# Attention and token mixture on one core: every mixture product and attention score as one float32 matmul, without the split into halves

## The chip, the core and the metric

The kernel runs on one core of a Trainium2 chip. The metric is the device time of the whole program in microseconds (us). Five engines matter: TensorE (PE in the profile; PEld is its loading of the stationary operand), VectorE (DVE), ScalarE (ACT), GpSimd (POOL) and SyncE (SP, which here only issues transfers).

## The reference

Eight batches, eight heads each, 576 tokens, head size 64. Attention keeps only the scores within `tau` of the row's maximum; its output `x` (576 x 512 per batch) goes through a mixture that turns each channel by an angle, mixes tokens, and adds a clipped channel product.

```python
scores = scale * np.matmul(q, k.transpose(0, 1, 3, 2))
thresh = np.max(scores, axis=-1, keepdims=True) - tau
scores = np.where(scores >= thresh, scores, -1000000000.0)
attn = np.exp(scores - max); attn = attn / (sum(attn) + 1e-09)
x = attn @ v                          # heads side by side: (8, 576, 512)
theta = x @ w_theta
y = w_tok_r @ (x * cos(theta)) + w_tok_i @ (x * sin(theta))
u = x + y
out = u + np.maximum(u @ w_ch, 0.0)
```

All inputs are float32 or float64 and the results float32; the mixture's weights and scores have to be held to nearly float32 accuracy.

## The kernel before

**Attention.** Two heads make a pair; there are 32 pairs, four to a batch. A pair is cut into nine *halves*: for query blocks i = 0 to 3 of 128 rows one half for each of the two heads, and one half for the 64 last rows of both heads together (i = 4). `score` computes one half: 128 queries against 576 keys, in two pieces of 288 columns (`h`), into one PSUM tile `s_ps` of which there is a single buffer. VectorE then negates it into SBUF and takes the row minimum (`sc`, L282), ScalarE takes the exponential (L299), and VectorE masks it and sums the rows (L300). `flip` and `flip_last` turn the result with TensorE transposes (`t_ps`), ScalarE copies it out (`a`), and `values` multiplies it with `v` into `o_ps`, with the two heads in the two halves of the output partitions (64 columns of the array each). `invert` and `normalize` bring 1/sum to the layout of `xT` by five transposes (`rb_ps`, `rl_ps`) and VectorE multiplies.

**Operands in two parts.** TensorE's operands for scores, products and token sums are of type fp32r, and each float32 operand is split into a high part (a cast) and a low part (the rest). A key gives `k1`, `k2`; a query has its high part in partitions 0 to 63 and its low part in 64 to 127 of one tile, so that two matmuls give all four products of parts. Every product of the mixture is three matmuls: high x high, low x high, high x low.

```python
def split(eng_hi, eng_lo, hi, lo, src):
    copy(eng_hi, hi, src)
    eng_lo.tensor_tensor(out=lo, in0=src, in1=hi.bitcast(F32), op=ALU.subtract)
...
terms = ((0, 0), (1, 0), (0, 1))                      # product: 12 matmuls for each h
...
work = [(zz[c][0], w[:, c, hs]) for c in range(NK) for w in (wt_h, wt_l)]
work += [(zz[c][1], wt_h[:, c, hs]) for c in range(NK)]   # token: 27 matmuls for each h
```

**Mixture.** `moe(b)` works on blocks m = 0 to 3 of 128 channels: `angle` (a product with `w_theta`, then VectorE reduces the angle: `km`, L453), `sines` (ScalarE sine and cosine for two m at once, between two table loads, and GpSimd multiplies them with `x`, L483), `flip` (nine transposes for each m), `token` (`y_ps`), and four products with `w_ch`. The string `ORDER` sets their sequence. `split_x` and `split_u` split `x` and `u`; the split weights of the products lie in DRAM and are fetched again by a GpSimd DMA for each m.

**Order of the work.** TensorE runs in the order in which the code is written. `score` is called three halves ahead. After each score and after each flip, `fill()` puts in pieces of the mixture of the batch before, as many as a cost budget allows (`share` per call, less the number that each piece yields). So there are nine stretches: the attention of batch 0 alone, with the conversion of the weights (`load_weight`: float64 to float32 on ACT, DVE and PE); then seven rounds of one batch's attention with the mixture of the batch before; and the last mixture alone. The other engines' order is set by a list scheduler, by priorities and its own estimate of the times.

Of the kernel before, what the change touches and what calls it, by code (L numbers as in the profile page):

```python
# [10 lines left out]
F32 = mybir.dt.float32  # L11
F32R = mybir.dt.float32r
# [4 lines left out]
DRAM = bass.MemoryType.DRAM  # L17
# [16 lines left out]
LAG = 3  # L34
# [5 lines left out]
def tile_attn_moe(  # L40
# [12 lines left out]
    B, NP, D, _, S = qT.shape  # L53
# [4 lines left out]
    SP = S + 64  # L58
    NK = 9
# [3 lines left out]
    dram = ctx.enter_context(tc.tile_pool(name="dram", bufs=1, space=DRAM))  # L63
# [27 lines left out]
    wt_h = const.tile([P, NK, S], F32R, name="wt_h")  # L91
    wt_l = const.tile([P, NK, S], F32R, name="wt_l")
    wm_dram = dram.tile([2, NM, P, 2, NM, P], F32, name="wm_dram")

    def pool_copy(out, in_):
        nc.gpsimd.tensor_scalar(out=out, in0=in_, scalar1=1.0, scalar2=0.0, op0=ALU.mult, op1=ALU.add)

    def copy(eng, out, in_):
        if eng is nc.scalar:
            nc.scalar.copy(out=out, in_=in_)  # L100
        elif eng is nc.gpsimd:
            pool_copy(out, in_)
        else:
            eng.tensor_copy(out=out, in_=in_)  # L104

    def split(eng_hi, eng_lo, hi, lo, src):

        copy(eng_hi, hi, src)
        eng_lo.tensor_tensor(out=lo, in0=src, in1=hi.bitcast(F32), op=ALU.subtract)  # L109
# [10 lines left out]
    turn = [0]  # L120

    def load_weight(src, n, on_pe=True):

        w = pool.tile([P, S], F32, tag="xh", name="w", bufs=4)[:, :n]
        if src.dtype == F32:
            nc.sync.dma_start(w, src)
            yield
            return [(slice(0, n), w)]
        turn[0] += 1
        tag, bufs = ("wm", 3) if turn[0] % 2 else ("z", 3)  # L130
        raw = pool.tile([P, S, 2], U32, tag=tag, name="wraw", bufs=bufs)[:, :n]
        nc.sync.dma_start(raw, src.bitcast(U32).rearrange("p (n t) -> p n t", t=2))
        low, high = raw[:, :, 0], raw[:, :, 1]
        bits = pool.tile([P, S], U32, tag="xh", name="bits", bufs=4)[:, :n]
        mag = pool.tile([P, S], U32, tag="xl", name="mag", bufs=4)[:, :n]
# [11 lines left out]
        nc.vector.tensor_scalar(out=mag, in0=bits, scalar1=0xFF800000, scalar2=None, op0=ALU.bitwise_and)  # L147
        nc.vector.scalar_tensor_tensor(out=w, in0=low, scalar=2.0**-52, in1=magf, op0=ALU.mult, op1=ALU.mult)
        if not on_pe:
            nc.vector.tensor_tensor(out=w, in0=w, in1=bitsf, op=ALU.add)  # L150
            yield
            return [(slice(0, n), w)]
# [3 lines left out]
        got = []  # L156
        for c in range(0, n, n2):
# [3 lines left out]
            got.append((slice(c, c + n2), ps))  # L161
        return got

    def load_wtok(c):
        got = yield from load_weight(w_tok[c * P : (c + 1) * P, :], S)
        for r, w in got:
            split(nc.scalar, nc.vector, wt_h[:, c, r], wt_l[:, c, r], w)

    def load_wm(which, src, c):
        got = yield from load_weight(src[c * P : (c + 1) * P, :], DM, which == 0)  # L170
        hi, lo = (pool.tile([P, DM], F32R, tag="zh4" if x == "whi" else "zl4", name=x, bufs=4) for x in ("whi", "wlo"))
        for r, w in got:
            split(nc.scalar, nc.vector, hi[:, r], lo[:, r], w)
        for i, t in enumerate((hi, lo)):
            nc.sync.dma_start(
                wm_dram[which, :, :, i, c, :].rearrange("m p e -> p m e"),
                t.bitcast(F32).rearrange("p (m e) -> p m e", e=P),
            )
# [11 lines left out]
    def get_wm(which, m):  # L190
# [19 lines left out]
    def load_raw(n, src, name, j):  # L210
        raw = temp(name)
        for r in (slice(0, 64), slice(64, P)):
            nc.sync.dma_start(raw[r], src[n // NP, n % NP, :, j])
# [486 lines left out]
```

## Time and profile before

| | |
|---|---|
| median of 3 runs | 1151.37 us (1150.37 to 1155.16) |
| span of the profiled execution | 1147.4 us |
| around the span (median less span) | 4.0 us |
| TensorE busy | 1043.9 us, 91% |
| VectorE busy | 869.0 us, 76% |
| ScalarE busy | 750.0 us, 65% |
| GpSimd busy | 375.1 us, 33% |
| mean granted TensorE clock | 0.981 |
| mean DMA rate | 92 GB/s |

No own time of the profiled execution is given beside its span; it is taken as the span and the 4.0 us that the median lies above it.

How to read it: matmuls are pipelined, and a matmul's shown duration (around 0.3 us) contains its passage through the array; what one costs TensorE is the distance to the next start. In the chain of waits, pieces of consecutive matmuls follow each other without overlap, so that a piece's time over its count is that distance. The list of groups by line shows a matmul once for each instruction that TensorE executed; a matmul on float32 operands is two instructions there, one on fp32r is one.

### The profile page before, as it was taken

The numbers are of one execution on the slowest core, as the hardware profiler recorded it, in microseconds if no ns is written. First come the engines' busy times: TensorE is split into PE (matmuls) and PEld (weight loads), VectorE is DVE, ScalarE is ACT, GpSimd is POOL, SyncE is SP. The second block draws the span as 40 slices with busy tenths as digits, with TensorE's granted clock in tenths as the row PEclk, the third lists the DMA queues.
The fourth block names the chain that finished last, engine by engine and source line by source line (L and its number), as shares of the span: only waits on it lengthen the run. The fifth ranks groups of instructions, "written<-read, shape, count | busy, mean of one in ns | idle before, by whom it ended". The sixth has DMA issues, their size and how long they took to land.

```text
span 1147.4 us, 21175 instructions
## 1 busy us (share of the span) xinstructions
PE 1043.9 (91%) x7736; PEld 921.5 (80%) x7736; DVE 869.0 (76%) x2139; ACT 750.0 (65%) x1394; POOL 375.1 (33%) x303
## 2 busy tenths in 40 slices
PE   4888888799899998999979998999989999799998
PEld 3566687688779987898869987799878998689898
DVE  7998777987877677876787768776788678787362
ACT  6766869666676566964677666865678656774350
POOL 2203325233342243521443234422435314430210
PEclk9999999999999998999999999999999999999999
DMA  7722223255231052213432142311522133310421
GB/s 252 213 81 84 64 71 97 88 138 148 76 100 53 28 178 74 79 47 103 116 100 63 32 146 76 102 53 34 173 87 72 43 113 104 97 32 1 120 71 60
DMA packets 55176, 105.26 MB, mean 92 GB/s; under 512 B 11936, under 2 KB 20128, under 8 KB 55072
## 3 DMA queue, kind: packets, MB, share of 16 engines
q1 hardware_dynamic: 45856, 70.35, 20.9%
q0 software_dynamic: 9216, 33.56, 10.2%
q8 instruction: 61, 1.00, 0.4%
q14 instruction: 43, 0.35, 0.1%
HBM read 90.24 MB, written 13.63 MB: 91 GB/s over the span
## 4 chain that ended last, share of the span: by engine, by line
PE 64%; DVE 15%; ACT 13%; issue 4%; DMA 2%; POOL 1%; SPq 0%; ACTq 0%; POOLq 0%; DVEq 0%
PE y_ps L512 15%; PE m_ps L405 13%; PE o_ps L361 13%; PE s_ps L278 11%; PE t_ps L326 7%; DVE sc L282 3%; DVE s_sb L300 3%; DVE km L453 3%; ACT s_sb L299 3%; DMA qraw<-in_qT_dram 2%; ACT a L331 2%; PE rb_ps L377 1%; PE z_ps L495 1%; ACT z L471 1%; ACT z L472 1%
## 5 line engine op out<-in xcount | busy, mean ns | idle before, releaser
L300 DVE SCALAR_TENSOR_TENSOR s_sb<-sc,nm,s_sb 128x576 f32<-128x576 f32 x288 | 276.1, 960 | 69.4 <-ACT s_sb L299 65.5
L299 ACT ACTIVATE s_sb<-sc,nm 128x576 f32<-128x576 f32 x288 | 224.1, 778 | 110.8 <-DVE sc L282 109.9
L278 PE MATMUL s_ps<-k,qq 128*128 128x288 f32 (+1 forms) x1344 | 240.2, 307 | 53.8 <-DVE sc L282 39.8
L282 DVE TENSOR_SCALAR_CACHE_REDUCE sc<-s_ps 128x576 f32<-128x576 f32 x288 | 216.7, 753 | 67.2 <-PE s_ps L278 64.3
L278 PEld LDWEIGHTS s_ps<-k,qq 128*128 128x128 f32 x1344 | 193.8, 192 | 81.4 <-DVE sc L282 46.6
L361 PE MATMUL o_ps<-a,v 128*64 128x320 f32 (+1 forms) x1280 | 180.2, 430 | 31.2 <-DVE nm L295 27.7
L331 ACT COPY a<-t_ps 128x512 f32<-128x512 f32 x256 | 148.2, 579 | 58.2 <-PE t_ps L326 56.9
L326 PE MATMUL t_ps<-ident,s_sb 128*128 128x128 f32 x1152 | 175.4, 275 | 1.7 <-DVE zl L498 1.7
L361 PEld LDWEIGHTS o_ps<-a,v 128*64 128x64 f32 x1280 | 92.5, 143 | 97.8 <-ACT s_sb L299 30.4
L512 PE MATMUL y_ps<-wt_h,zh 128*128 128x288 f32 x576 | 165.2, 305 | 6.3 <-DVE zl L498 4.8
L512 PE MATMUL y_ps<-wt_l,zh 128*128 128x288 f32 x576 | 163.0, 301 | 0.0
L109 POOL TENSOR_TENSOR k<-kraw,k 128x576 fp32r<-128x576 f32 x62 | 90.8, 1465 | 202.4 <-ACT k L100 201.0
L228 POOL TENSOR_TENSOR qq<-qraw,qq 64x576 fp32r<-64x576 f32 x62 | 95.1, 1534 | 159.9 <-ACT qq L226 130.4
L326 PEld LDWEIGHTS t_ps<-ident,s_sb 128*128 128x128 f32 x1152 | 142.4, 142 | 3.8 <-DVE zl L498 1.9
L512 PEld LDWEIGHTS y_ps<-wt_h,zh 128*128 128x128 f32 x576 | 108.6, 188 | 8.1 <-DVE zl L498 6.2
L512 PEld LDWEIGHTS y_ps<-wt_l,zh 128*128 128x128 f32 x576 | 108.6, 189 | 0.0
L512 PE MATMUL y_ps<-wt_h,zl 128*128 128x288 f32 x576 | 103.6, 306 | 0.0
L192 POOL DMA_DIRECT2D wm<-wm_dram x64 | 36.4, 570 | 171.0 <-PE m_ps L405 142.6
L405 PE MATMUL m_ps<-xh,wm 128*128 128x288 f32 x512 | 91.5, 305 | 0.3 <-ACT xh L100 0.3
L483 POOL TENSOR_TENSOR z<-z,xT 128x576 f32<-128x576 f32 x56 | 80.0, 1457 | 31.5 <-ACT z L471 31.4
L109 POOL TENSOR_TENSOR ul<-xT,uh 128x576 fp32r<-128x576 f32 x24 | 34.7, 1448 | 169.8 <-DVE uh L104 169.8
L405 PE MATMUL m_ps<-uh,wm 128*128 128x288 f32 x512 | 84.0, 299 | 0.0
(85 smaller groups left out, 1641.9 us busy)
## 6 DMA issues: line engine op xcount, KB each, us to landing
wm<-wm_dram POOLq DMA_DIRECT2D x64, 512.0 KB, 4.0
qraw<-in_qT_dram SPq DMA_DIRECT2D x128, 144.0 KB, 2.9
kraw<-in_kT_dram SPq DMA_DIRECT2D x128, 144.0 KB, 2.9
out_dram<-xT SPq DMA_DIRECT2D x32, 288.0 KB, 2.2
v<-in_vp_dram SPq DMA_DIRECT2D x32, 256.0 KB, 2.7
wraw<-in_w_tok_dram SPq DMA_DIRECT2D x9, 576.0 KB, 5.0
wraw<-in_w_theta_dram SPq DMA_DIRECT2D x4, 512.0 KB, 4.4
wm_dram<-whi SPq DMA_DIRECT2D x8, 256.0 KB, 2.3
```

The lines of the kernel that those rows point to most:

```text
L109: eng_lo.tensor_tensor(out=lo, in0=src, in1=hi.bitcast(F32), op=ALU.subtract)
L228: eng.tensor_tensor(out=qq[64:128], in0=raw[64:128], in1=qq[64:128].bitcast(F32), op=ALU.subtract)
L278: nc.tensor.matmul(ps[:, h, d0:d1], st, kk, start=(x == 0), stop=(x == len(todo) - 1))
L282: nc.vector.tensor_scalar(out=sc.rearrange("p (a b) -> p a b", a=2), in0=ps[:, :, :HS], scalar1=-1.0, scalar2=None, op0=ALU.mult, op1=ALU.min,
L299: nc.scalar.activation(out=e, in_=u.ps[j], func=AF.Exp, bias=nm[:, j : j + 1], scale=-1.0)
L300: nc.vector.scalar_tensor_tensor(out=e, in0=u.ps[j], scalar=nm[:, 2 + j : 3 + j], in1=e, op0=ALU.is_le, op1=ALU.mult, accum_out=u.pr.rows[ ...
L326: nc.tensor.transpose(out=tp[:, c * P : (c + 1) * P], in_=u.sf[:, k0 + c * P : k0 + (c + 1) * P], identity=ident)
L331: nc.scalar.copy(out=t.a[:, :, j, q0 : q0 + P], in_=tp.rearrange("p (c q) -> p c q", c=4))
L361: nc.tensor.matmul(o[64 * j : 64 * j + 64, :w], st, mv, start=(c == 0), stop=(c == 4))
L405: nc.tensor.matmul(tiles[h][:, :HS], wm[:, a, c, :], parts[c][bb][:, hs], start=(count[h] == 0), stop=(count[h] == 11))
L483: lo_eng.tensor_tensor(out=zi, in0=zi, in1=x, op=ALU.mult)
L512: nc.tensor.matmul(ps[:, :HS], z, w, start=(n == 0), stop=(n == len(work) - 1))
```

## The change

- `score`: the two heads' keys lie stacked in the 128 partitions of one float32 tile `k` (the second head's turned by 64 columns, as before), and a query tile holds one head's queries in its 64 partitions and zeros in the other 64. One float32 matmul per `h` replaces two fp32r matmuls. For i = 4, whose query columns hold both heads, a second key tile `k4` with both heads' keys unturned is loaded.
- `prepare_q`, `prepare_k`: transfers go straight into these tiles; of the splits only the scaling of the queries by `gate` stays, on ScalarE (one instruction for both heads).
- `product`, `token`: one float32 matmul for each block instead of three fp32r ones: 4 instead of 12, and 9 instead of 27. `split`, `split_x`, `split_u`, the low parts `zl`, the weights' trip through DRAM and `get_wm` go; the weights `wt`, `wm` stay in SBUF in float32.
- `normalize`: the copy `rb` on ScalarE goes; ten float32 matmuls of 64 columns spread 1/sum instead of five transposes of 128 columns, and one VectorE multiply instead of two closes the last columns.
- The costs that `fill` counts: 242 for each float32 matmul in place of 131 for each fp32r one; `share` follows.

```diff
 def load_weight(src, out, on_pe=True):
...
             nc.tensor.matmul(ps, ident, bitsf[:, c : c + n2], start=True, stop=False)
             nc.tensor.matmul(ps, ident, w[:, c : c + n2], start=False, stop=True)
-            got.append((slice(c, c + n2), ps))
+            nc.scalar.copy(out=out[:, c : c + n2], in_=ps)
 def load_wtok(c):
-        for r, w in got:
-            split(nc.scalar, nc.vector, wt_h[:, c, r], wt_l[:, c, r], w)
+        yield from load_weight(w_tok[c * P : (c + 1) * P, :], wt[:, c])
...
+    def prepare_q(n):
+        pr = pairs[n] = SimpleNamespace(n=n, b=n // NP, p=n % NP, a={})
+        pr.qf = qq_t[n % 2]
+        for j in range(2):
+            r = slice(64 * j, 64 * j + 64)
+            mine = pr.qf[r, S * j : S * j + S]
+            nc.sync.dma_start(mine, qT[pr.b, pr.p, j])
...
+            nc.scalar.activation(out=pr.qf, in_=pr.qf, func=AF.Copy, scale=gate)
+    def prepare_k(n):
+        pr.k = pool.tile([P, S], F32, tag="k", name=f"k{n}", bufs=3)
+        nc.sync.dma_start(pr.k, kT[pr.b, pr.p, 0:2].rearrange("j d s -> (j d) s"))
+        pr.k4 = pool.tile([P, S], F32, tag="k4", name=f"k4{n}", bufs=2)
+        for j in range(2):
+            nc.sync.dma_start(pr.k4[64 * j : 64 * j + 64], kT[pr.b, pr.p, 2 * j])
...
 def score(u, j):
-            parts = [(pr.qf[:, c : c + P], j, kk, 0) for kk in pr.keys[j]]
...
-                nc.tensor.matmul(ps[:, h, d0:d1], st, kk, start=(x == 0), stop=(x == len(todo) - 1))
+        c = 512 if u.i == 4 else u.i * P + SP * j
+        k = pr.k4 if u.i == 4 else pr.k
         for h in range(2):
+            nc.tensor.matmul(ps[:, h, :HS], pr.qf[:, c : c + P], k[:, h * HS : (h + 1) * HS], start=True, stop=True)
...
 def normalize(pr):
-        for i in range(4):
-            nc.tensor.transpose(out=tp[:, i * P : (i + 1) * P], in_=pr.rb[:, i * P : (i + 1) * P], identity=ident)
+        for i in range(5):
+            for j in range(2):
+                r = slice(64 * j, 64 * j + 64)
+                if i < 4:
+                    out, col, eye = tp[r, i * P : (i + 1) * P], 2 * i + j, ident
+                else:
+                    out, col, eye = tl[r, :64], 8, ident[:, r]
+                nc.tensor.matmul(out, pr.rows[:, col : col + 1].broadcast_to([P, 64]), eye, start=True, stop=True)
...
 def product(w, m, xs, todo, together):
-            runs = [[(h, *t, c) for t in terms for c in range(NM)] for h in range(2)]
+            runs = [[(h, c) for c in range(NM)] for h in range(2)]
...
-                    yield 131 * (len(run) if len(run) < 12 else 4)
+                if n == len(run) - 1 or n % 2 == 1:
+                    yield 242 * (n % 2 + 1)
...
 def flip(m):
-                nc.scalar.copy(out=zh, in_=tv)
-                nc.vector.tensor_tensor(out=zl, in0=tv, in1=zh.bitcast(F32), op=ALU.subtract)
+                nc.scalar.copy(out=zt[:, c0 : c0 + nb], in_=tp[:, : nb * P].rearrange("p (c q) -> p c q", q=P))
 def token(m):
-                for n, (z, w) in enumerate(work):
-                    nc.tensor.matmul(ps[:, :HS], z, w, start=(n == 0), stop=(n == len(work) - 1))
-                    if n % 3 == 2:
-                        yield 393
+                for c in range(NK):
+                    nc.tensor.matmul(ps[:, :HS], zt[:, c], wt[:, c, hs], start=(c == 0), stop=(c == NK - 1))
+                    if c % 2 == 1 or c == NK - 1:
+                        yield 242 * (1 + c % 2)
...
-    share = (16 * 3 * 524 + 4 * 990 + 72 * 393) / (per - 1) / 2
+    share = (64 * 242 + 4 * 990 + 72 * 242) / (per - 1) / 2
```

How the order moves, at two places on which the prediction rests.

TensorE, in a round, while one block's `token` runs between the scores and flips of the attention. Before, a score is four rows and the token sum alternates between the weights' two parts; the step shown ends at the next score:

```order
L278 MATMUL s_ps<-k_15_0_5752,qq_85 128x288
L278 MATMUL s_ps<-k_15_0_5753,qq_85 128x288
L278 MATMUL s_ps<-k_15_0_5752,qq_85 128x288
L278 MATMUL s_ps<-k_15_0_5753,qq_85 128x288
L512 MATMUL y_ps<-wt_h,zh 128x288
L512 MATMUL y_ps<-wt_l,zh 128x288
L512 MATMUL y_ps<-wt_h,zh 128x288
L512 MATMUL y_ps<-wt_l,zh 128x288
L512 MATMUL y_ps<-wt_h,zh 128x288
L512 MATMUL y_ps<-wt_l,zh 128x288
L512 MATMUL y_ps<-wt_h,zh 128x288
L512 MATMUL y_ps<-wt_l,zh 128x288
```

The same engine in the same kind of place after the change:

```order
L221 MATMUL s_ps<-k_3920,qq_81 128x288 x2
L430 MATMUL y_ps<-wt,zt 128x288 x3
L269 MATMUL t_ps<-ident,s_sb 128x128 x4
L284 MATMUL t_ps<-ident,s_sb 128x128
L430 MATMUL y_ps<-wt,zt 128x288 x2
L221 MATMUL s_ps<-k_3920,qq_81 128x288 x2
```

The sequence of scores, mixture pieces and flips is the same; a score is two written matmuls, and four or five token matmuls stand in a step where there were about fifteen. Over the whole program the matmuls of 288 columns go from 1216 (and 64 pairs of 224 and 64 columns), 1536 and 1728 for scores, products and token sums to 576, 512 and 576.

VectorE, in the attention of batch 0 after the weights are done (pair 3; `sc` is a score leaving PSUM, `s_sb` the masked exponential, `nm` a small instruction on the row minimum). Before, the score of the next half stands ahead of the mask of this one:

```order
L282 TENSOR_SCALAR sc,nm<-s_ps 128x576
L300 SCALAR_TENSOR_TENSOR s_sb,rows_1095<-sc,nm,s_sb 128x576
L295 TENSOR_SCALAR nm<-nm,small 128x1
L282 TENSOR_SCALAR sc,nm<-s_ps 128x576
L300 SCALAR_TENSOR_TENSOR s_sb,rows_1095<-sc,nm,s_sb 128x576
L295 TENSOR_SCALAR nm<-nm,small 128x1
L282 TENSOR_SCALAR sc,nm<-s_ps 128x576
L300 SCALAR_TENSOR_TENSOR s_sb,rows_1095<-sc,nm,s_sb 128x576
```

The same engine and place after the change:

```order
L225 TENSOR_SCALAR sc,nm<-s_ps 128x576
L238 TENSOR_SCALAR nm<-nm,small 128x1
L243 SCALAR_TENSOR_TENSOR s_sb,rows_632<-sc,nm,s_sb 128x576
L225 TENSOR_SCALAR sc,nm<-s_ps 128x576
L238 TENSOR_SCALAR nm<-nm,small 128x1
L243 SCALAR_TENSOR_TENSOR s_sb,rows_632<-sc,nm,s_sb 128x576
L225 TENSOR_SCALAR sc,nm<-s_ps 128x576
L238 TENSOR_SCALAR nm<-nm,small 128x1
```

After the change, each half's three instructions follow each other, so that VectorE stands in its queue before the mask until ScalarE has this half's exponential. The same pattern holds in most of the rounds.

More of the change, by code (lines that the diff above doesn't have):

```diff
@@ L52, in tile_attn_moe @@
     nc = tc.nc
-    B, NP, D, _, S = qT.shape
+    B, NP, _, D, S = qT.shape
     P = 128
@@ L58, in tile_attn_moe @@
     SP = S + 64
+    assert D == 64 and S == 576
     NK = 9
@@ L89, in tile_attn_moe @@
     nc.vector.memset(half_pi, 0.5 * math.pi)
[L91 to L109, printed above, removed]
+    wt = const.tile([P, NK, S], F32, name="wt")
+    wm = [const.tile([P, NM, DM], F32, name=f"wm{i}") for i in range(2)]
     def temp(name, dt=F32):
@@ L160, in load_weight @@
             nc.tensor.matmul(ps, ident, w[:, c : c + n2], start=False, stop=True)
-            got.append((slice(c, c + n2), ps))
-        return got
+            nc.scalar.copy(out=out[:, c : c + n2], in_=ps)
     def load_wtok(c):
-        got = yield from load_weight(w_tok[c * P : (c + 1) * P, :], S)
-        for r, w in got:
-            split(nc.scalar, nc.vector, wt_h[:, c, r], wt_l[:, c, r], w)
+        yield from load_weight(w_tok[c * P : (c + 1) * P, :], wt[:, c])
     def load_wm(which, src, c):
[L170 to L178, printed above, removed]
+        yield from load_weight(src[c * P : (c + 1) * P, :], wm[which][:, c], which == 0)
     def all_loads(todo):
@@ L382, in normalize, with product @@
         x = xT[pr.n]
         nc.vector.tensor_tensor(out=x[:, :512], in0=x[:, :512], in1=tp, op=ALU.mult)
-        for j in range(2):
-            r = slice(64 * j, 64 * j + 64)
-            nc.vector.tensor_tensor(out=x[r, 512:S], in0=x[r, 512:S], in1=tl[r, 64 * j : 64 * j + 64], op=ALU.mult)
-    def product(wm, parts, todo, together):
-        terms = ((0, 0), (1, 0), (0, 1))
+        nc.vector.tensor_tensor(out=x[:, 512:S], in0=x[:, 512:S], in1=tl[:, :64], op=ALU.mult)
+    def product(w, m, xs, todo, together):
@@ L405, in product @@
                 nc.tensor.matmul(
[L406 removed]
+                    tiles[h][:, :HS],
+                    w[:, c, m * P : (m + 1) * P],
+                    xs[c][:, hs],
+                    start=(count[h] == 0),
+                    stop=(count[h] == NM - 1),
                 )
                 count[h] += 1
[L409 removed]
+                if count[h] == NM:
                     todo(tiles[h], hs)
[L411 to L426 removed]
+                if n == len(run) - 1 or n % 2 == 1:
+                    yield 242 * (n % 2 + 1)
     def moe(b):
@@ L432, in moe @@
         lo_eng = nc.vector if last else nc.gpsimd
-        xs = parts.pop(b)
+        xs = [xT[b * NP + c] for c in range(NM)]
         zs = {}
@@ L448, in evict @@
                     )
[L450 removed]
+            yield from product(wm[0], m, xs, evict, m == 0)
             km = temp("km")
@@ L537, in moe @@
                     yield cost
-                left -= 1
             elif what == "s":
@@ L605, in begin @@
             invert(u.pr)
-    for j in range(2):
-        prepare_q(0, (j,))
-        prepare_k(0, j)
+    prepare_q(0)
+    prepare_k(0)
     load_v(0)
@@ L642, in tile_attn_moe @@
                 if (i, j) == (1, 0):
-                    for jj in range(2):
-                        prepare_k(n + 1, jj)
+                    prepare_k(n + 1)
                 if i == 4:
```

158 lines of the change are left out of this document (36 added, 122 removed).

## The prediction

> **What bounds the kernel now.** I read the page's busy shares first, then the span cut into stages: the start, the attention of batch 0 with the weights, its end, three rounds, one round alone, three more, the last mixture.
>
> ```profile
> PE 1043.9 (91%) x7736; PEld 921.5 (80%) x7736; DVE 869.0 (76%) x2139; ACT 750.0 (65%) x1394; POOL 375.1 (33%) x303
> ...
> 20.00:111.60 91.60, 74.22 (x413) 54.57 (x413) 86.05 (x210) 59.19 (x117) 20.19 (x16) 0.96 0.48 143
> 111.60:148.80 37.20, 29.49 (x210) 22.25 (x210) 29.87 (x90) 31.49 (x62) 13.02 (x9) 1.00 0.23 65
> 148.80:556.60 407.80, 379.50 (x2869) 339.35 (x2869) 315.51 (x780) 277.45 (x516) 145.88 (x113) 0.97 0.32 93
> 556.60:689.70 133.10, 124.83 (x959) 111.76 (x958) 101.77 (x252) 91.06 (x170) 48.66 (x39) 0.99 0.30 86
> 689.70:1081.20 391.50, 368.96 (x2829) 330.47 (x2827) 293.33 (x726) 259.12 (x486) 131.33 (x105) 0.99 0.27 79
> 1081.20:1147.40 66.20, 60.07 (x446) 58.30 (x444) 30.98 (x60) 18.83 (x30) 12.11 (x12) 0.99 0.23 71
> ```
>
> Columns: length, then PE, PEld, DVE, ACT, POOL, clock. Up to 111.6 us VectorE is busy 94% (86.05 of 91.60): it bounds batch 0's stage. In the seven rounds, 932.4 us in all, TensorE is busy 94% (124.83 of 133.10), VectorE 76%, ScalarE 68%. Four fifths of the kernel are TensorE's. What a matmul costs there, from the chain of waits (whose pieces do not overlap) and from the timeline, where starts follow each other:
>
> ```profile
> 55.19 2.84 PE o_ps L361 x20
> 432.83 0.52 PE s_ps L278 x4
> 1130.79 12.75 PE m_ps L405 x96
> 104.73 0.65 PE L159 MATMUL w_ps<-bits,ident 128*128 128x288 f32 x2
> 105.22 0.65 PE L160 MATMUL w_ps<-w,ident 128*128 128x288 f32 x2
> 105.70 0.49 PE L326 MATMUL t_ps<-ident,s_sb 128*128 128x128 f32 x3
> 502.57 0.60 PE L326 MATMUL t_ps<-ident,s_sb 128*128 128x128 f32 x4
> 503.00 0.27 PE L341 MATMUL t_ps<-ident,s_sb 128*128 128x128 f32 x1
> ```
>
> An fp32r matmul of 288 columns costs 12.75/96 = 0.133 us (a score, 0.52/4 = 0.130). The weight conversion is the one place with a float32 matmul of the new shape, 128 stationary columns by 288. One written matmul is two executed ones (x2), and the starts 104.73, 105.22, 105.70 stand 0.49 and 0.48 apart: **0.486 us for one written float32 matmul**, 3.65 times the fp32r one. Three fp32r matmuls cost 0.399, two 0.266. So each replacement is dearer on the engine that bounds.
>
> **The change on TensorE.** A batch's mixture has 8 products x 24 = 192 fp32r matmuls, now 64: 64 x 0.486 - 192 x 0.133 = 31.1 - 25.5 = +5.6 us. Its token sums have 8 x 27 = 216, now 72: 35.0 - 28.7 = +6.3. A batch has 36 halves, and their scores cost 160 x 0.133 = 21.3 (a 224 and a 64 column piece counted as one), now 72 x 0.486 = 35.0: +13.7. For `normalize` I price a new matmul by width from `o_ps`, whose instructions also use 64 array columns: 2.84/20 = 0.142 for 320 columns, so 0.057 for 128. Sixteen of these and four of half the width make 1.0 us, against five transposes at (503.00 - 502.57)/4 = 0.108, or 0.5: +0.5 a pair, +2 a batch. Its bounds are 0 (the old form's whole price, if they overlap better) and +2.3 a pair (20 at 0.142, if width saves nothing), +9 a round. A full round grows by 5.6 + 6.3 + 13.7 + 2.0 = **27.6 us; seven rounds, +193**.
>
> **What a round can give back.** Its waits on TensorE, and the stall behind the largest:
>
> ```profile
> PE o_ps L361 <- DVE nm L295: 4.5, 1, 4.5
> PE s_ps L278 <- DVE sc L282: 3.6, 4, 1.6
> PE y_ps L512 <- DVE zl L498: 0.8, 1, 0.8
> ...
> 575.54 5.52 POOL L483 TENSOR_TENSOR z<-z,xT 128x576 f32<-128x576 f32 x4
> 575.94 5.45 DVE L453 TENSOR_SCALAR km<-th 128x576 f32<-128x576 f32 x1
> ...
> 440.90 5.43 DVE km L453
> 575.94 5.45 DVE km L453
> 709.03 5.45 DVE km L453
> ...
> 582.00:587.00 5.00, 3.75 (x18) 2.03 (x20) 3.67 (x11) 2.12 (x4) 0.00 (x0) 0.66 0.24 59
> ```
>
> Taking every matmul at these prices, the round of 133.1 holds about 119 of TensorE work and 14 of idle. A third is one event that returns every round: `km`, beside four multiplications on GpSimd, lasts 5.45 us, VectorE's queue stands still, TensorE waits 4.5, and then the clock falls to 0.66 over 5 us, which costs 1.7 more. The change leaves these multiplications and `km` where they were, so I keep this 6 us. The waits on `sc` and `zl`, 4.4 together, I take as gone: `zl` no longer exists, and VectorE and ScalarE lose
>
> ```profile
> L498 DVE TENSOR_TENSOR zl<-z_ps,zh 128x512 fp32r<-128x512 f32 x64 | 43.5, 681 | 5.7 <-ACT zh L497 5.7
> L109 DVE TENSOR_TENSOR wt_l<-w_ps,wt_h 128x288 fp32r<-128x288 f32 x18 | 7.9, 446 | 0.9 <-ACT wt_h L100 0.8
> L109 DVE TENSOR_TENSOR wlo<-w_ps,whi 128x512 fp32r<-128x512 f32 x4 | 2.7, 668 | 0.0
> L225 ACT ACTIVATE qraw<-qraw,small 128x576 f32<-128x576 f32 x64 | 49.7, 778 | 28.0 <-DMA qraw<-in_qT_dram 27.5
> L226 ACT CAST qq<-qraw 128x576 fp32r<-128x576 f32 x64 | 43.0, 671 | 0.3
> L100 ACT CAST k<-kraw 128x576 fp32r<-128x576 f32 x64 | 43.2, 675 | 25.6 <-PE s_ps L278 23.5 <-DMA kraw<-in_kT_dram 1.9
> ```
>
> (the query scaling shrinks, its casts and the keys' go) while a round gets longer. With 0.6 of the small rest, 5 us a round: -35. This has bounds too: 0, if other waits take their place, and -14, if all idle goes, -98 over seven rounds. I stay near the middle because the named event alone holds 6.
>
> **The other stages.** Batch 0: TensorE's +15.7 lies beside VectorE, busy 86 of 91.6. VectorE loses wt_l 7.9, wlo 2.7 and, at the 0.759 of a key's split (last row below), 3 for the four splits of the first pair, 14 in all. But its order now runs half by half:
>
> ```profile
> L300 DVE SCALAR_TENSOR_TENSOR s_sb<-sc,nm,s_sb 128x576 f32<-128x576 f32 x288 | 276.1, 960 | 69.4 <-ACT s_sb L299 65.5
> L299 ACT ACTIVATE s_sb<-sc,nm 128x576 f32<-128x576 f32 x288 | 224.1, 778 | 110.8 <-DVE sc L282 109.9
> L282 DVE TENSOR_SCALAR_CACHE_REDUCE sc<-s_ps 128x576 f32<-128x576 f32 x288 | 216.7, 753 | 67.2 <-PE s_ps L278 64.3
> L331 ACT COPY a<-t_ps 128x512 f32<-128x512 f32 x256 | 148.2, 579 | 58.2 <-PE t_ps L326 56.9
> L295 DVE TENSOR_SCALAR nm<-nm,small 128x1 f32<-128x1 f32 x288 | 59.5, 207 | 3.0
> L282 DVE DVE_READ_ACCUMULATOR sc<-s_ps 128x1 f32 x288 | 23.6, 82 | 0.0
> L471 ACT ACTIVATE z<-z,small 128x576 f32<-128x576 f32 x32 | 24.7, 772 | 0.3
> L467 ACT ACT_TABLE_LOAD x16 | 20.5, 1283 | 0.3
> L109 DVE TENSOR_TENSOR k<-kraw,k 128x576 fp32r<-128x576 f32 x2 | 1.5, 759 | 0.1
> ```
>
> A serial half takes 0.753 + 0.778 + 0.960, with two accumulator reads of 0.08 and hand-overs some 2.7 us, against 2.08 of VectorE's own time with `nm`. Behind the waiting mask stand the next `sc` and, since `s_ps` has one buffer, TensorE's next score; over the last two pairs' 18 halves, where no weight work fills the gap, I charge 9 of the possible 13. Net -5; bounds -14 and +12. If the cover is gone, TensorE's 15.7 comes out instead. The last mixture is TensorE's alone: +11.9, less 2 for the splits between its steps: +10. The GpSimd work that goes (splits, weight fetches) I cost at nothing: none of a round's waits on TensorE quoted above names it. The query transfers now go into a tile that the scores of two pairs earlier have read, so on SP they wait for these, with weight and value loads behind them; they are issued some six halves ahead of their first use, 24 us at the new pace, so I cost this at nothing too. If that cover failed, ScalarE would wait as it does for `qraw` now, 27.5 us over 64 scalings.
>
> **Sum**, in the span: 1147.4 + 193 - 35 - 5 + 10 = 1310; with the 4.0 around it, **1314 us**, 14% above the median of 1151.37.
>
> **Rivals.**
> *Half the price (faster).* If a float32 matmul in a dense stream cost 0.243, as the new cost table counts it, a round's 208 would take 50.5 instead of 75.5: -25, -23 with `normalize`, and -5 of waits. With -11 in the last mixture and -10 in batch 0 the span is 1147 - 7 x 28 - 21 = 930, though VectorE's 102 a round would hold it at about 980. It decides below (75.5 + 3)/208 = 0.38 us. For it speaks the table alone; against it, 104.73 to 105.70. Chance 4%. The Trainium skill's "Perfetto Trace Analysis" (Engine Utilization) halves TensorE's output rate for FP32_LOW_HIGH, an estimate of 0.24 us, whereas "FP8 and Floating Point Precision" (TensorE Precision Notes) gives true FP32 four passes, 0.48; the rows agree with the second, if one executed instruction is two passes, which they do not show.
>
> *VectorE's serial order becomes the bound.* In a round 36 halves x 2.7 = 97, other VectorE work 102 - 36 x 2.08 - 6 (`zl`) = 21, `km` 5 more: 123. If each exponential also queues behind one ScalarE copy of 0.58, 144; with ScalarE held twice a round by four sines and two table loads (4 x 0.772 + 2 x 1.283 = 5.6), 155, level with TensorE's own 147. Each further 0.2 us of waiting for an exponential adds 7 a round: 162 to 170 a round, 1355 to 1405. Against it speaks that the copies fit into ScalarE's third of idle time. Chance 15%.
>
> *The idle goes.* TensorE being slower, `km` comes later than the four multiplications, and the stall goes with its half clock: 6 more a round, 1272. Chance 18%. The skill's "TensorE: Matmul & The Clock Gate" (Part 1) halves the clock after an idle window of about 3.4 us; by that rule a stall cut to 3 us alone would save the 1.7 a round, 1302, and the row with 0.66 agrees with the fall.
>
> **Numbers.** My forecast has 62%; 1% is left for no change. Faster 0.04, same 0.01, slower 0.95, with 0.5% as what a measurement here can tell from none. The range takes in the vanished idle below and part of the serial order and the dearer `normalize` above: 1266 to 1365.
>
> **What will show it.** Executed matmuls of 288 columns 0.243 apart in scores, products and token sums; a round of about 156 us with TensorE busy over 93%; one long `km` a round; batch 0 done near 144. It is wrong if starts lie 0.12 apart, if TensorE waits on `sc` or `s_sb` for over 15 us a round, or if `normalize` takes over 2 us a pair.

## The result: 1290.57 us, 12% slower

The changed kernel takes 1290.57 us (median of four runs, 1289.7 to 1293.0) against 1151.16 (four runs; the 1151.37 above is of three): 1.1205 times the time before, with a 95% interval of 1.1184 to 1.1226. The forecast was 1314, with 1266 to 1365 as its range; of the forecast's rise of 163 us, 139 came.

First the page after: the busy shares, then the three groups of float32 matmuls (busy time, mean ns of one executed instruction, idle time ahead of them and what ended it).

```profile
PE 1238.6 (96%) x6936; PEld 932.5 (72%) x6936; DVE 721.7 (56%) x1925; ACT 654.0 (51%) x1189; POOL 84.3 (7%) x69
...
L221 PE MATMUL s_ps<-k,qq 128*128 128x288 f32 x1152 | 343.6, 421 | 34.5 <-DVE sc L225 28.1 <-ACT qq L181 6.4
L430 PE MATMUL y_ps<-wt,zt 128*128 128x288 f32 x1152 | 321.9, 407 | 9.8 <-ACT zt L419 9.8
L342 PE MATMUL m_ps<-xT,wm 128*128 128x288 f32 x1024 | 280.9, 407 | 3.1 <-ACT a L287 3.1
```

VectorE lost 147 us of work, ScalarE 96, GpSimd 291, and the kernel is slower all the same: TensorE has fewer instructions and 195 us more to do. In 1289.6 us of span it waits 47 in these three groups.

The same span by stages, cut as before at the first products (length, then PE, PEld, DVE, ACT, POOL, clock):

```profile
20.00:111.60 91.60, 81.26 (x433) 56.62 (x431) 68.97 (x181) 51.51 (x101) 0.00 (x0) 0.98 0.28 88
111.60:157.70 46.10, 36.78 (x232) 25.76 (x233) 28.43 (x85) 25.59 (x50) 0.00 (x0) 1.00 0.17 46
157.70:616.30 458.60, 451.42 (x2569) 342.13 (x2568) 264.69 (x709) 240.73 (x436) 34.68 (x24) 1.00 0.15 44
616.30:768.20 151.90, 149.88 (x858) 113.86 (x857) 84.77 (x229) 79.42 (x144) 11.59 (x8) 1.00 0.14 40
768.20:1215.90 447.70, 441.23 (x2529) 334.87 (x2528) 243.66 (x655) 230.17 (x420) 34.70 (x24) 1.00 0.11 33
1215.90:1289.60 73.70, 70.08 (x309) 54.86 (x307) 21.21 (x41) 17.61 (x28) 0.00 (x0) 1.00 0.06 21
```

| stage | before | forecast | after |
|---|---|---|---|
| batch 0, to the first product | 148.8 | 144 | 157.7 |
| seven rounds | 932.4 | 1090 | 1058.2 |
| last mixture | 66.2 | 76 | 73.7 |
| span | 1147.4 | 1310 | 1289.6 |

One round of the middle is 151.9 against 133.1, and the clock in the rounds is 1.00 where 0.97 to 0.99 stood. What the float32 matmuls cost is read from TensorE's timeline, where a row's start less the next row's start is the distance:

```profile
674.32 1.14 PE L430 MATMUL y_ps<-wt,zt 128*128 128x288 f32 x4
675.29 1.13 PE L221 MATMUL s_ps<-k,qq 128*128 128x288 f32 x4
676.26 0.60 PE L418 MATMUL z_ps<-ident,z 128*128 128x128 f32 x4
...
685.00 1.04 PE L322 MATMUL rb_ps<-ident,rows 128*64 128x128 f32 x16
685.87 0.28 PE L322 MATMUL rl_ps<-ident,rows 128*64 128x64 f32 x4
686.09 1.24 PE L221 MATMUL s_ps<-k,qq 128*128 128x288 f32 x4
```

Four executed instructions, which are two written matmuls, take 0.97 us in the token sum and 0.97 in the score: 0.243 for an executed one, 0.486 for a written one. The new `normalize` takes 686.09 - 685.00 = 1.09 us a pair. TensorE's waits in this whole round are three (total, times, longest):

```profile
PE y_ps L430 <- ACT zt L419: 1.3, 1, 1.3
PE s_ps L221 <- DVE sc L225: 0.4, 1, 0.4
PE m_ps L342 <- ACT a L287: 0.3, 1, 0.3
```

The wait of 4.5 for `nm`, which came behind the long `km`, is not among them.

### The profile page after: what moved, and what is told of

Read it like the earlier page. It is cut to its first block, busy times and chain, and to the rows that moved or that the text cites. A ratio compares the mean times of both kernels' runs of the same rounds, so it can differ in the third digit from the quotient of the medians.

```text
span 1289.6 us, 18359 instructions
## 1 busy us (share of the span) xinstructions
PE 1238.6 (96%) x6936; PEld 932.5 (72%) x6936; DVE 721.7 (56%) x1925; ACT 654.0 (51%) x1189; POOL 84.3 (7%) x69
## 4 chain that ended last, share of the span: by engine, by line
PE 77%; ACT 15%; DMA 4%; DVE 3%; issue 1%; SPq 1%; ACTq 0%
PE y_ps L430 19%; PE s_ps L221 18%; PE m_ps L342 14%; PE o_ps L304 13%; PE t_ps L269 7%; DMA qq<-in_qT_dram 3%; ACT s_sb L242 2%; PE rb_ps L322 2%; ACT z L396 2%; DVE sc L225 2%; PE z_ps L418 2%; ACT L401 1%; ACT L396 1%; ACT L242 1%; ACT a L274 1%; ACT z L397 1%
## 5 line engine op out<-in xcount | busy, mean ns | idle before, releaser
L221 PE MATMUL s_ps<-k,qq 128*128 128x288 f32 x1152 | 343.6, 421 | 34.5 <-DVE sc L225 28.1
L243 DVE SCALAR_TENSOR_TENSOR s_sb<-sc,nm,s_sb 128x576 f32<-128x576 f32 x288 | 246.1, 854 | 181.2 <-ACT s_sb L242 180.3
L430 PE MATMUL y_ps<-wt,zt 128*128 128x288 f32 x1152 | 321.9, 407 | 9.8 <-ACT zt L419 9.8
L221 PEld LDWEIGHTS s_ps<-k,qq 128*128 128x128 f32 x1152 | 211.8, 192 | 110.5 <-DVE sc L225 37.4
L342 PE MATMUL m_ps<-xT,wm 128*128 128x288 f32 x1024 | 280.9, 407 | 3.1 <-ACT a L287 3.1
L430 PEld LDWEIGHTS y_ps<-wt,zt 128*128 128x128 f32 x1152 | 206.6, 190 | 57.4 <-ACT zt L419 12.4
L342 PEld LDWEIGHTS m_ps<-xT,wm 128*128 128x128 f32 x1024 | 186.3, 190 | 48.3 <-ACT a L287 4.8
L419 ACT COPY zt<-z_ps 128x512 f32<-128x512 f32 (+1 forms) x96 | 46.2, 483 | 78.4 <-PE z_ps L418 78.1
L238 DVE TENSOR_SCALAR nm<-nm,small 128x1 f32<-128x1 f32 x288 | 61.1, 212 | 7.7
L183 ACT ACTIVATE qq<-qq,small 128x1152 f32<-128x1152 f32 x31 | 38.9, 1256 | 44.6 <-DMA qq<-in_qT_dram 37.1
L418 PE MATMUL z_ps<-ident,z 128*128 128x128 f32 x288 | 47.1, 273 | 0.0
```

The lines of the kernel that those rows point to most:

```text
L221: nc.tensor.matmul(ps[:, h, :HS], pr.qf[:, c : c + P], k[:, h * HS : (h + 1) * HS], start=True, stop=True)
L238: nc.vector.tensor_scalar(out=nm[:, 2 + j : 3 + j], in0=nm[:, j : j + 1], scalar1=span, scalar2=None, op0=ALU.add)
L243: nc.vector.scalar_tensor_tensor(out=e, in0=u.ps[j], scalar=nm[:, 2 + j : 3 + j], in1=e, op0=ALU.is_le, op1=ALU.mult, accum_out=u.pr.rows[ ...
L342: nc.tensor.matmul(tiles[h][:, :HS], w[:, c, m * P : (m + 1) * P], xs[c][:, hs], start=(count[h] == 0), stop=(count[h] == NM - 1),)
L418: nc.tensor.transpose(out=tp[:, i * P : (i + 1) * P], in_=z[:, c : c + P], identity=ident)
L430: nc.tensor.matmul(ps[:, :HS], zt[:, c], wt[:, c, hs], start=(c == 0), stop=(c == NK - 1))
```

## Where the round's idle time went

Each executed instruction of a round, counted at its row's price (0.243 for float32 and 0.133 for fp32r at 288 columns, 0.109 for a transpose; for the 64-column matmuls of `o_ps` and `normalize` 0.135 at 320 columns, their spacing in a dense stretch, and less by width), gives TensorE's work; the rest of the round is idle:

| | work | idle | round |
|---|---|---|---|
| before | 119.0 | 14.1 | 133.1 |
| after | 146.2 | 5.7 | 151.9 |

Work rose by 27.2 where 27.6 was forecast; as a count at row prices it shows that the counts and the spacing came out as forecast, and nothing of the waits. Idle fell by 8.4 where 5 was forecast. By the spacing of the starts, the idle ahead of `o_ps`, where the stall behind `km` stood, fell by about 6.4, that ahead of the scores by 2.1, and that ahead of the token sums rose by 0.4. The stall is gone because `km` is never long now. The timeline of VectorE, ScalarE and GpSimd in this round, only the rows of `km`, of the loads and activations around it and of the multiplications:

```profile
633.12 0.46 DVE L378 TENSOR_SCALAR km<-th 128x576 f32<-128x576 f32 x1
...
635.11 1.24 ACT L397 ACTIVATE z<-th 128x576 f32<-128x576 f32 x2
635.28 4.14 POOL L408 TENSOR_TENSOR z<-z,xT 128x576 f32<-128x576 f32 x3 [126.11 <-ACT z L396]
636.36 1.28 ACT L242 ACT_TABLE_LOAD   x1
...
637.66 0.78 ACT L242 ACTIVATE s_sb<-sc,nm 128x576 f32<-128x576 f32 x1
...
638.93 1.28 ACT L396 ACT_TABLE_LOAD   x1
640.22 0.78 ACT L396 ACTIVATE z<-z,small 128x576 f32<-128x576 f32 x1
640.45 0.46 DVE L378 TENSOR_SCALAR km<-th 128x576 f32<-128x576 f32 x1
...
641.07 1.90 POOL L408 TENSOR_TENSOR z<-z,xT 128x576 f32<-128x576 f32 x1 [1.65 <-ACT z L396]
```

ScalarE slips one exponential between the sines, which costs two more table loads (636.36 and 638.93) and holds up the fourth sine to 640.22. So GpSimd does three of the group's four multiplications, stops for 1.65 us, and does the fourth from 641.07. The second `km` starts at 640.45, 7.3 us after the first, in that gap, and lasts 0.46. Before, it started 3.96 after the first, with the four multiplications running back to back, and lasted 5.45 until they had all ended.

## Experiments

### Scores back to fp32r

Only the scores go back to two fp32r matmuls on split operands; products, token sums and `normalize` stay in float32.

```diff
-        qq = const.tile([P, 2 * S], F32, name=f"qq{i}")
+        qq = const.tile([P, S + SP], F32R, name=f"qq{i}")
...
+            eng.tensor_tensor(out=k2, in0=raw, in1=k1.bitcast(F32), op=ALU.subtract)
...
 def score(u, j):
-            nc.tensor.matmul(ps[:, h, :HS], pr.qf[:, c : c + P], k[:, h * HS : (h + 1) * HS], start=True, stop=True)
+            for x, (st, d0, d1, kk) in enumerate(todo):
+                nc.tensor.matmul(ps[:, h, d0:d1], st, kk, start=(x == 0), stop=(x == len(todo) - 1))
```

> The changed kernel with the attention scores alone put back: queries and keys split into two fp32r parts, two fp32r matmuls for each float32 one. Theory (TensorE's prices set the round): 72 x 0.486 - 160 x 0.133 = 13.7 us less a round, seven rounds, 1290.6 - 96 = about 1195, and batch 0 (bound elsewhere) changes by less than 5. Rival 1 (the idle came back): TensorE's steps are short again, km meets the multiplications on GpSimd, 6 us a round of the gain are lost, about 1237, with km instructions of 5 us in the trace. Rival 2 (VectorE's serial order bounds the rounds): a round stays near 148, above 1260.

Measured: 1228.68 us, 1.0681 [1.066, 1.0702] times before, 62 us less than the changed kernel. One round of it, and its largest wait over the span:

```profile
588.40:731.50 143.10, 138.80 (x882) 109.79 (x881) 88.01 (x228) 87.17 (x163) 35.87 (x24) 0.99 0.17 50
```

```profile
PE y_ps L450 <- DVE xT L453: 15.4, 7, 2.4
```

The round has 132.5 of work, the 13.7 less that the prices give; the fp32r rows of the scores stand 0.133 apart here too. But idle is 10.6, up by 4.9. TensorE reaches the first token sum sooner and waits there 2.4 us in this round, where the changed kernel waits 1.3; `o_ps` waits 1.4 that it did not wait there, and the clock falls again. So scores in float32 cost 14 a round of work, and 9 in time. The expected 1195 was missed by 34. The time is near the first rival's 1237, but not by its mechanism: no `km` lasts over 1.46 us.

### Token sums back to fp32r

```diff
-                    nc.tensor.matmul(ps[:, :HS], zt[:, c], wt[:, c, hs], start=(c == 0), stop=(c == NK - 1))
+                    for q3, (z, w) in enumerate(((zh, wt_h), (zh, wt_l), (zl, wt_h))):
+                        nc.tensor.matmul(
+                            ps[:, :HS], z[:, c], w[:, c, hs], start=(c == 0 and q3 == 0), stop=(c == NK - 1 and q3 == 2)
+                        )
```

The splits of the weights and of `z` come back with it, on VectorE, and `z` has three buffers instead of four.

> The changed kernel with the token sums alone put back: each float32 matmul becomes three fp32r ones in the same place, with the low parts made by VectorE; the buffers of z go from four to three to make room. Theory (TensorE's prices): 216 x 0.133 against 72 x 0.486, 6.3 us less a mixture, eight mixtures, about 1240; batch 0 gets up to 8 us longer by the split of the weights on VectorE. Rival (idle comes back, the km stall of 6 a round): about 1282. If a float32 matmul cost half in the dense stream the time would rise instead, by 8 x 11 = 88, to 1380.

Measured: 1255.70 us, 1.092 [1.0886, 1.0954] times before, 35 less than the changed kernel. One round:

```profile
606.90:753.50 146.60, 144.06 (x929) 116.74 (x928) 89.36 (x241) 79.34 (x144) 11.63 (x8) 1.00 0.14 41
```

Its work is 139.9, the 6.3 less that the prices give, its idle 6.7, one more. The last mixture is 68.1, 5.6 less: there the price shows in time. Batch 0 is 166.7, 9 longer, with the weights' split on VectorE again; up to 8 was expected. Without these 9 it would be 1247, near the expected 1240.

### The mask after the next score

The changed kernel with VectorE's old order: a half's mask behind the next half's `sc`.

```diff
     def begin(n, i, j):
-        score(u, j)
+        sc = score(u, j)
+        if waiting:
+            after(mask(*waiting.pop()), sc)
         softmax(u, j)
+        waiting.append((u, j))
```

> The changed kernel with VectorE's order as before the change: each half's masked exponential is written after the next half's score has left PSUM. Nothing else moves. Theory (the serial order made batch 0 longer): the first product starts at about 145 instead of 157.7, the rounds keep 152, so 1278, 1.0% faster. Rival 1 (TensorE's dearer scores and the one PSUM buffer of scores bound batch 0): batch 0 stays within 3 us, 1290. Rival 2 (the later mask makes the flips wait): rounds grow by over 2 us, above 1300.

Measured: 1277.44 us, 1.1104 [1.1075, 1.1133] times before, 13 less. Batch 0 and the seven rounds:

```profile
0.00:150.00 150.00, 126.54 (x678) 86.50 (x679) 104.67 (x293) 84.84 (x161) 3.37 (x13) 0.99 0.33 101
150.00:1203.10 1053.10, 1040.44 (x5952) 790.86 (x5951) 566.98 (x1591) 531.85 (x986) 80.68 (x56) 1.00 0.13 39
```

Batch 0 fell from 157.7 to 150.0, the rounds by 5 in all. So the serial order is worth 7.7 us in batch 0 and 0.7 a round. The total is the expected 1278, but by luck in its parts: some 13 were expected from batch 0 and nothing from the rounds. Batch 0 also varies: in two runs below whose batch 0 has the changed kernel's TensorE sequence (the sines together, and the multiplications on VectorE) it ends at 161.6 and 161.9, so that a difference there is good to some 4 us. What the serial order does in batch 0 is seen in the changed kernel's timeline, pair 3:

```profile
127.37 1.24 PE L221 MATMUL s_ps<-k,qq 128*128 128x288 f32 x4 [0.31 <-DVE sc L225]
127.62 0.79 ACT L242 ACTIVATE s_sb<-sc,nm 128x576 f32<-128x576 f32 x1
128.44 0.82 DVE L243 SCALAR_TENSOR_TENSOR s_sb<-sc,nm,s_sb 128x576 f32<-128x576 f32 x1 [0.88 <-ACT s_sb L242]
129.19 0.75 DVE L225 TENSOR_SCALAR_CACHE_REDUCE sc<-s_ps 128x576 f32<-128x576 f32 x1
130.00 1.24 PE L221 MATMUL s_ps<-k,qq 128*128 128x288 f32 x4 [0.96 <-DVE sc L225]
```

The score starting at 127.37 is done by 128.6, but VectorE has stood 0.88 us for the exponential and now runs the mask; `sc` follows at 129.19, and only its end frees the one `s_ps`, so that the next score starts at 130.00 after 0.96 of waiting. The whole span's wait of scores on `sc`, 28.1 in the group of L221 above, is 19.1 in this run.

### The multiplications in the kernel before, from GpSimd to VectorE

This asks whether the 5.45 us of `km` is GpSimd's doing, in the kernel before.

```diff
-        lo_eng = nc.vector if last else nc.gpsimd
+        lo_eng = nc.vector
```

> The kernel before, with the multiplications of sine and cosine by x on VectorE in all batches, as it already is in the last one, instead of GpSimd. Theory (the km instruction of 5.45 us stands behind the four GpSimd multiplications and costs the round 6 us with the half clock): no km over 1 us, rounds of 127, 1151 - 42 = about 1109. Rival (VectorE's eight multiplications of 0.75 a round, 6 us, come into the path in their place): within 1% of 1151.

Measured: 1130.66 us, 0.9832 [0.9808, 0.9856] times before: 21 us less, where 42 were expected. `km` (shortest, median, longest in ns) and the largest wait that came:

```profile
L453 DVE TENSOR_SCALAR km<-th x32: 448/459/556, 156.5 to 1079.8; 128x576 f32<-128x576 f32 x32
```

```profile
PE z_ps L495 <- DVE zl L498: 6.9, 8, 1.5
```

The long `km` is gone, and the waits of `o_ps` for `nm` with it, 27.7 over the span before. Half of its price came back as other waits: 6.9 of `z_ps` for `zl` (1.6 before), 5.4 of `o_ps` for `a`, 3.8 of scores for GpSimd's key parts. A round shortened by 3 us, from an average of 133.2 to 130.2.

### Keeping the sines together

In the changed kernel the four sines are tied together, without the exponential between them, the second block's first. The edit also takes out the early load of the sine table, which stood ahead of them.

```diff
-            ahead_of = after(nc.scalar.preload_act_table(AF.Sin), ab)
...
-                for m, th, z in todo:
-                    ins = [
+                ins = []
+                for m, th, z in reversed(todo):
+                    ins += [
...
-                    for x in ins:
-                        after(x, ahead_of)
+                for x in ins[1:]:
+                    after(x, ins[0])
```

> The changed kernel with the four sines of two blocks kept together on ScalarE: no exponential of the attention can slip between them, so that a group has two table loads instead of four in most cases (14 of 16 groups were torn). Theory (the round is 146 us of TensorE work and 6 of idle, and the torn sines are the 1.5 us wait of the token sum on ScalarE's copy): 1.0 to 1.5 us a round less, 1290 - 9 = about 1281. Rival (the km stall went away in the changed kernel only because the torn sines spread the four GpSimd multiplications): km instructions of about 5 us return, 6 us a round more, about 1325.

Measured: 1303.88 us, 1.1329 [1.1301, 1.1357] times before: 13 us slower than the changed kernel, where 9 less was expected. The rival's `km` of 5 us did not come either: the longest is 1.70. Its new wait on TensorE, and a window behind that wait in one round (length, busy times, clock in the seventh column):

```profile
PE z_ps L418 <- POOL z L408: 14.9, 7, 2.3
```

```profile
651.00:656.00 5.00, 4.58 (x20) 3.10 (x22) 2.71 (x7) 1.88 (x4) 2.25 (x2) 0.66 0.00 0
```

TensorE flips the first block first, and its sines now come last: a round waits 2.1 us at `z_ps` on average, up to 2.3, and after four of the seven waits the clock falls as in this window. Four table loads a round are saved, on an engine that is busy 51%. What the later load of the sine table adds was not separated. Two more runs used the same edit. On the kernel with fp32r scores:

> The kernel with the scores in fp32r halves (1228.7, where 1195 was expected), with the sines kept together as in the run beside it. Its round was 143.1, of which 132 are TensorE work and 10.8 idle; the largest wait stood behind ScalarE's torn sines. Theory: the idle falls to about 6, the round to 138, the time to 1229 - 34 = 1195, the price worked out for the scores. Rival (the idle comes from GpSimd's splits beside VectorE, or from the km stall): within 8 us of 1229, or above it.

It took 1229.34 us (1.0684 [1.0653, 1.0714]), no less than without it. The waits of `o_ps`, 10.3 us over the span, were gone, but the wait ahead of the token sums had moved in part to the flips and doubled:

```profile
PE z_ps L438 <- POOL z L428: 16.4, 7, 2.4
PE y_ps L450 <- ACT zt L439: 13.1, 7, 2.2
```

And on the kernel before, with the multiplications left on GpSimd, to see whether the torn sines or the multiplications make `km` long:

> The kernel before with the sines kept together alone; the multiplications stay on GpSimd. Theory: km still lasts 5 us beside them, so 1151 less at most 10. Rival (the torn sines, not the multiplications, are what the stall of 4.5 us on TensorE waits for): the stall goes, about 1115.

It took 1173.49 us, 1.0191 [1.0158, 1.0225] times before: 22 us more, which neither expected. `km` and the new wait:

```profile
L453 DVE TENSOR_SCALAR km<-th x32: 449/460/5449, 158.5 to 1126.4; 128x576 f32<-128x576 f32 x32
```

```profile
PE z_ps L495 <- POOL z L483: 14.4, 7, 2.6
```

With the sines together `km` still lasts 5.449 us, and with the multiplications on VectorE (the section before) at most 0.556: the multiplications make it long.

### Both edits in the kernel before, in two orders

With the multiplications on VectorE and the sines together, second block first, as in the diffs above:

> The kernel before with the multiplications on VectorE (1130.7) and the sines kept together. Theory: seven of sixteen groups were torn, 2.6 us of ScalarE each; TensorE, at 118.8 of work in a round of 129.7, gets back up to 2 us a round, about 1120. Rival (VectorE's queue is what the rounds wait for now): 1131.

1125.27 us, 0.9774 [0.9746, 0.9802], midway between the two; `z_ps` waits 10.7 us over the span for the multiplications. Then with the first block's sines first, in the order in which TensorE flips:

```diff
-            for m in ms:
+            for m in reversed(ms):
...
-                todo.append((m, th, z))
+                todo.insert(0, (m, th, z))
```

> The kernel before with the multiplications on VectorE (1130.7) and the sines kept together, the first block's first. With the second block's first it was 1125.3, with 10.7 us of waits of the flips for the multiplication. Theory: these waits go, about 1113. Rival: other waits take them, 1125.

1113.78 us, 0.9673 [0.965, 0.9697] times before: the fastest of all, 3.3% under the kernel before. Its steady round:

```profile
542.90:670.50 127.60, 123.65 (x957) 111.03 (x957) 99.11 (x260) 87.66 (x168) 37.28 (x31) 1.00 0.30 90
```

TensorE's matmuls are those of the kernel before, 119.0 at the same prices, so the idle is 9 instead of 14, with all products still split.

### The same edits on the kernel with fp32r scores, and on the changed kernel

Whether the waits that kept the first experiment from its 1195 can be removed: fp32r scores with the multiplications on VectorE, and then also with the sines together, first block first.

> The kernel with the scores in fp32r halves (1228.7), with the multiplications by x on VectorE instead of GpSimd. Theory (with shorter steps TensorE reaches the flips and token sums before the path sine, multiplication of 1.45 us on GpSimd, flip, copy has brought their operand; 10.8 us of a round idle): a multiplication of 0.75 shortens that path, the round falls from 143 to about 139, the time to about 1200. Rival (the path is ScalarE's torn sines alone): no change, 1229. Rival (VectorE's added 6 us a round fill its queue): above 1235.

> As the run beside it, and the sines of two blocks kept together with the first block's first, so that its multiplications and flips come first. Theory (both halves of the path cost): idle falls to 6 of the round as in the changed kernel, round 138, about 1195, the price of the scores on TensorE in full. Rival (the wait moves on again, as it did when the sines alone were kept together): 1215 to 1230.

1223.33 us (1.0622 [1.0593, 1.0652]) and 1226.07 us (1.0636 [1.0613, 1.0659]), 5 and 3 us less than without, far from 1195 to 1200; of the expectations, the second run's rival, that the wait moves on, is what came. The wait at the first token sum, in the one and the other:

```profile
PE y_ps L450 <- DVE xT L453: 22.7, 7, 3.3
```

```profile
PE y_ps L450 <- ACT zt L439: 23.1, 7, 3.6
```

It is 3.3 us a round either way. Last, the changed kernel with its multiplications on VectorE:

> The changed kernel with the multiplications by x on VectorE. Theory (TensorE's 146 us of work set the round of 152; GpSimd beside VectorE costs at most the 1.4 us wait of the token sum): 1280 to 1290. Rival (contention of GpSimd and VectorE still costs 3 us a round as it did before the change): about 1268.

1291.36 us, 1.1209 [1.1182, 1.1236]: no change. Its wait at the token sum is the changed kernel's, to the digit:

```profile
PE y_ps L430 <- ACT zt L419: 9.8, 7, 1.9
```

So moving GpSimd's multiplications gains the changed kernel nothing: no stall of theirs on TensorE was left in it to remove.

## Why the prediction was right, and where it was off

**How near it was.** Of the sum's parts the rounds came out 32 us below the forecast, batch 0 14 above, the last mixture 2 below, which leaves 20 in the span. That the total is so near is in part luck, since the two large errors have opposite signs. In the rounds alone, the rival that the idle goes (42 us less) was 10 off, nearer than the forecast.

**The price.** The step that carried the forecast held: 0.486 us for a written float32 matmul in a dense stream. A round's work grew by 27.2 (27.6 forecast). With the scores and the token sums taken back singly, the rows stood at the prices of the forecast, 13.7 and 6.3 a round; in time, the token sums gave 5.6 in the last mixture, where hardly any idle time stands between them. The products' 5.6 were not taken back alone. The half price, which would have shown starts 0.12 apart, fell; the 980 that I gave as VectorE's limit there does not follow from its sum, since VectorE's 102 a round lie below the 105 a round that the sum gives. On the two pages of the Trainium skill that differ here: the estimate from "FP8 and Floating Point Precision" (TensorE Precision Notes), four passes, agrees with 0.97 for four executed instructions, which are two written matmuls; that from "Perfetto Trace Analysis" (Engine Utilization), a halved rate, is half of what the trace shows for a written matmul, and what it shows for an executed one.

**`normalize`.** 1.09 a pair against 1.0: the price by width from `o_ps` was good.

**What a round gives back: mis-sized.** I kept 9 us of idle in each round, 6 of them the stall behind `km` with its slow clock, because the change leaves those instructions in place. They stayed, but their distance changed, and the stall went as the rival said. Idle fell to 5.7, so that the seven rounds came out 32 us below the forecast, 4.6 a round on average: 3.4 of idle, 0.4 of work, and the rest mostly from the first three rounds, which took 8.5 more than three middle ones before (407.8 against 3 x 133.1) and 2.9 more after (458.6 against 3 x 151.9). The rival's mechanism was half right: the second `km` does come later, but it does not come after the four multiplications; it falls into a gap that a torn row of sines opens. The gap is not what keeps it short, though: with the sines together and no gap it lasted at most 1.70. What moves it from 3.96 to 7.3 us is not settled. VectorE's order is not all of it: with the old order the longest `km` was 1.53 us, still no 5 us event.

**Batch 0: wrong sign.** I forecast -5; it was +9. I charged 9 for the serial order and credited 14 for splits that VectorE no longer does. The order cost 7.7, as the run with the old order shows, near the charge (whose possible 13 should read 11: 18 halves at 2.7 less 2.08). The credit is what failed: with the old order batch 0 is still 150.0, one more than before, though VectorE is busy only 72 of the 91.6 us up to 111.6, against 86. VectorE's share there did not set that stage's end. What took its place was not separated: TensorE is busy 83.9 of these 91.6 us there, against 74.2 before, and a term that I put at nothing also stands in the way.

**The query transfers in batch 0: not nothing.** I costed them at nothing, because they are issued well ahead of the scores that use them. But their scaling stands in ScalarE's queue ahead of exponentials that are due sooner. ScalarE waits longer for them than for `qraw` before (37.1 us against 27.5), and the chain behind the score that starts at 119.84 runs through one transfer and its scaling:

```profile
ACT qq L183 <- DMA qq<-in_qT_dram: 37.1, 27, 3.0
```

```profile
111.28 3.02 DMA qq<-in_qT_dram
...
114.38 1.26 ACT qq L183
...
116.25 0.68 ACT s_sb L242
...
119.84 0.51 PE s_ps L221
```

That score waits 1.73 us. From 42 us on ScalarE stands so four times in batch 0, for 2.9, 1.6, 1.8 and 1.6 us, and with the old order for 2.2, 1.6, 1.6 and 2.9. In the middle round the waits are there too (up to 2.0), but none of TensorE's waits names them. No run moved the transfers or the scaling, so how much of batch 0 is theirs stays open.

**The last mixture.** 73.7 against 76: +7.5 instead of +10. At the row prices its matmuls stand there with little idle time between them, so of the 11.9 of added work 4.4 was paid by waits between the steps that went, where I allowed 2.

**The serial order as the bound of the rounds** fell: a steady round waits 0.4 us on `sc`, and the old order gains 0.7 a round. Its upper time was off by some 8: 170 a round, 14.2 above the forecast's 155.8, make 1413. It is right only for batch 0, where no mixture pieces fill the gaps.

**What stays open.** With fp32r scores TensorE waits two to three us a round at the first token sum whatever is done to the sines and the multiplications. The chain angle, sines, multiplication, flip, copy ends there, and which of its members is the limit, or whether calling the angle a step earlier in `ORDER` would remove the wait, was not tried. Nor was the rival that GpSimd's splits of queries and keys hold VectorE up there: they stayed on GpSimd in all four of these runs. Why one `km` waits for four multiplications in the kernel before, and for about one elsewhere (longest 1.46 with fp32r scores, 1.70 with the changed kernel's sines together), is open too.

## What to carry to other kernels

Price a float32 matmul with 128 stationary columns from a row: here 0.486 us for 288 moving columns against 0.133 for fp32r, so two or three fp32r matmuls on split operands are the cheaper form where TensorE bounds, as in these rounds, and splits on engines that have time to spare are not what to save. Part of such a gain can come back as waits: the scores' 14 us a round were worth 9. A stall that hangs on how far apart two instructions stand on different engines is a coincidence: any edit that stretches the round can dissolve or create it, so give both cases their weight, and expect back only part of a stall that is removed. When a row of dependent work is reordered on one engine, keep the order in which the next engine takes it: in the kernel before, the same edit was worth 11 us more with the first block first. And follow a transfer to the queue in which its result is handled: even when it lands well ahead of its use, what stands behind it in that queue can wait.

## What the runs showed of the hardware

**The clock can fall after shorter waits than I took, and the length of a wait alone does not decide it.** A wait of 2.3 us at `z_ps` was followed by 0.66 over 5 us, the same value as after the 4.5 us in the kernel before. A wait of 1.3 in the changed kernel left it at 1.00 (the window in which that wait ends, columns as before):

```profile
661.00:666.00 5.00, 4.51 (x28) 2.89 (x29) 2.02 (x5) 3.45 (x8) 0.02 (x1) 1.00 0.01 3
```

The prediction used the rule of the Trainium skill's "TensorE: Matmul & The Clock Gate" (Part 1), an idle window of about 3.4 us. The window of 0.66 in the run with the sines together does not agree with it: a stall cut to 3 us need not have lost its slow stretch. But not every such wait is followed by a fall. In the same run another wait of 2.3 us ends at 959.64, and with fp32r scores and the first block's sines first one of 3.4 ends at 485.5; the 5 us behind each (the first row from the one run, the second from the other) are at full clock:

```profile
959.70:964.70 5.00, 5.00 (x38) 3.25 (x40) 2.23 (x7) 1.82 (x4) 1.78 (x1) 1.00 0.00 0
485.50:490.50 5.00, 4.98 (x35) 3.53 (x36) 1.92 (x7) 4.74 (x10) 0.00 (x0) 1.00 0.14 40
```

In the trace of the run with the sines together, the falls behind these waits start at 498.23, 651.83, 805.43 and 1112.63 us and last 3.41 each; their distances of 153.6, 153.6 and 307.2 are 45, 45 and 90 times 3.413. So the falls lie on a fixed grid, and where a wait lies on it may decide; no run tested that.

**VectorE can stand still behind a whole row of GpSimd instructions.** A `km` of 0.46 us lasted 5.45 beside four multiplications back to back. The Trainium skill's "SBUF — State Buffer" (SBUF: two separate sides) tells of a port pair that GpSimd shares with some of VectorE's operations by an exclusive lock, held for a whole instruction; whether `km` is one of them, no run here shows. The run with fp32r scores has a `km` that starts while the first multiplication runs, and lasts up to 1.456:

```profile
L398 DVE TENSOR_SCALAR km<-th x32: 452/460/1456, 161.2 to 1172.7; 128x576 f32<-128x576 f32 x32
```

That agrees with a lock of this kind; the 5.45 beside four is longer than a lock for one instruction explains.

**A torn pair of activation functions costs the load alone.** In the timeline of the changed round above, the two sines from 635.11 end at 636.35, the load runs from 636.36 for 1.28, and the exponential starts at 637.66: a switch between sine and exponential costs 1.30, with nothing else on ScalarE beside it.
